# Products that nobody reads, in an attention + mixture-of-experts + MLP kernel: eight beside the first loads, four at the first unit's scores, and one at most transposings of the first batch

## The chip, the cores and the metric

The kernel runs on one core of one Trainium2 chip. The metric is the device time of one execution in microseconds (us); lower is better. PE is TensorE's matmul side (PEld its weight loads), DVE is VectorE, ACT is ScalarE, POOL is GpSimd, SP is SyncE, whose queue (SPq) issues the DMAs.

## What is computed

Three stages follow each other, all in f32 to the outside. Attention has 2 batches, 8 heads, 576 positions and 64 channels; it adds a local attention (a band of 3 positions to either side) and a coarse attention on means of 4 positions, repeated 4 times. Its output, as 1152 rows of 512, goes through 8 experts with balanced gates, and then through an MLP.

```python
def sm_attn(qq, kk, vv):
    s = scale * np.matmul(qq, kk.transpose(0, 1, 3, 2))
    s = s - np.max(s, axis=-1, keepdims=True)
    a = np.exp(s)
    a = a / (np.sum(a, axis=-1, keepdims=True) + 1e-09)
    return np.matmul(a, vv)
out_d = sm_attn(q_d, k_d, v_d)                  # q, k, v averaged over 4 positions
out_up = np.repeat(out_d, factor, axis=2)
scores = np.where(np.abs(pos[:, None] - pos[None, :]) < factor, scale * q @ k.T, -1e9)
...
attn_out = out_up + out_local
...
for e in range(E):                              # 8 experts, P: balanced gates
    h = np.maximum(x @ w1[e], 0.0)
    out += P[:, e:e + 1] * (h @ w2[e])
...
h = x @ w_in
g = np.maximum(h, 0.0) + np.log1p(np.exp(-np.abs(h)))
return g @ w_out
```

## The kernel before

**Units and blocks.** The attention runs over eight units, each of one batch and two heads: units 0 to 3 are batch 0, units 4 to 7 batch 1 (`units`, L660; the first argument of `Unit(n, b, u)` is the running number `n`). A unit has four blocks: "c", the coarse attention, and 0, 1 and 2, each with three tiles of 64 positions of the local one.

**The steps of a unit.** `load` (L492) has SP issue the DMAs of q and k into one tile `qk` (one buffer, L494, so that the next unit's q and k can come only once this unit's have been transposed), of v into `vw` and `vd`. `setup(g)` (L514, g = 0, 1, 2) transposes three tiles of `qk` on PE (`tb`, L523) and has DVE and ACT copy and reduce them into `qkd`, `kT`, `fine` and, at g = 2, `flat`. `scores(blk)` (L551) takes a PSUM bank `sc` and computes the scores: for "c" from `flat` and `qkd` (L557), otherwise first the mask by one bf16 product of the identity `identb` with 216 columns (L564) and then three tiles (L570). DVE takes the maximum (L577), ACT the exponentials (L582), DVE normalises into `ex` (L583 to L585). `turn(blk)` (L588) takes a bank `tp`, transposes `ex` on PE (L596 for "c", which has two halves c and a bank for each; L605 for the others) and ACT copies it out. `values(blk)` (L609) multiplies with v into a bank `pv` (L616, L627); DVE adds the coarse part (L642).

**PSUM.** `bank` (L489, L66) gives out eight banks. In batch 0 scores take m0, m1 and m2 in turn, `tb` and `tp` share four banks with the tag "at", and `pv` has the one bank "y". In batch 1 all the attention's banks are the four "at" banks, and the others serve the experts' products.

**Order.** The loop at L1028 writes the blocks of all units as one stream: at step n it writes the scores of block n, in the last two blocks of a unit the next unit's setup and then its successor's load, then the turn of block n-2 and the values of block n-3 (`LAG` is 2). From half of the stream on it puts the experts' first products (L831, L919) between, and operands and weights are made ready on DVE, ACT and POOL. Up to here the order on each engine is made by the program's scheduler from this order and from its own estimate of what is ready; it is fixed when the program is built, and each engine runs its queue in that order. From L1097 on the experts and the MLP follow in an order written out by hand.

`ident` (f32, L95) and `identb` (bf16, L458) are identity matrices; DVE writes `identb` near the start.

The lines of the main loop before the stream starts, and those that place a block:

```python
    blocks = ["c", 0, 1, 2]
    stream = [(x, blk) for x in units for blk in blocks]
    for g in range(NB):
        units[0].setup(g)
    units[1].load()
    ...
            x.scores(blk)
            ...
        for lag, what in ((LAG, "turn"), (LAG + 1, "values")):
            if 0 <= n - lag < len(stream):
                x, blk = stream[n - lag]
                getattr(x, what)(blk)
```

Of the kernel before, what the change touches and what calls it, by code (L numbers as in the profile page):

```python
# [20 lines left out]
def attention_moe_mlp(ctx: ExitStack, tc: tile.TileContext, q, k, v, w_gate, w1, w2, w_in, w_out, out):  # L21
    nc = tc.nc
    B, H, S, D = q.shape
    NT, DM = out.shape
    E, _, FF = w1.shape
    F2 = w_out.shape[0]
    P = 128
# [92 lines left out]
    class Job:  # L120

        def __init__(self, steps, rank, pace=None):
            self.begun, self.pace = order_.now, pace
            self.steps, self.rank, self.want, self.active, self.taken, self.done = steps, rank, None, False, {}, set()
            self.last = 0.0
            self.go(None)
# [331 lines left out]
    identb = ap.tile([P, P], BF16, bufs=1, name="identb")  # L458
# [4 lines left out]
    for t0, t1, off in ((0, 1, 0), (1, NB + 1, R), (NB + 1, NB + 2, 2 * R)):  # L463

        for hh in range(2):
            part = mask[hh * QT : (hh + 1) * QT, t0:t1, :]
            for sign in (1, -1):
                nc.gpsimd.affine_select(
                    out=part, in_=part, compare_op=ALU.is_gt, fill=NEG,
# [6 lines left out]
    for x in fine + flat:  # L476
        nc.gpsimd.memset(x, 0.0)

    class Unit:


        pairs = {}

        def __init__(self, n, b, u):
            self.b, self.u = b, u
            self.flat = flat[n % 2]
            self.state = {}

# [62 lines left out]
        def scores(self, blk):  # L551

            sc = self.bank("sc", 0)
            if blk == "c":
                rows, w = 2 * CT, SD
                for i in range(NB):
                    nc.tensor.matmul(  # L557
                        sc[:rows, i * w : (i + 1) * w], self.flat[:, i].rearrange("x h q -> x (h q)"),
                        self.qkd[:, :, 1], start=True, stop=True,
                    )  # L560
            else:
                rows, w = P, KW
                tiles = range(NB * blk, NB * blk + NB)
                nc.tensor.matmul(  # L564
                    sc[:, : NB * w], identb, mask[:, blk : blk + NB].rearrange("p t w -> p (t w)"),
                    start=True, stop=False,
                )
                for i, t in enumerate(tiles):
                    w0 = min(max(t * QT - R, 0), S - KW)
                    nc.tensor.matmul(  # L570
                        sc[:, i * w : (i + 1) * w], fine[blk][:, i].rearrange("x h q -> x (h q)"),
                        self.kT.rearrange("x t q -> x (t q)")[:, w0 : w0 + KW], start=False, stop=(i == NB - 1),
                    )
            scv = sc[:rows, : NB * w].rearrange("p (i s) -> p i s", i=NB)
            small = ap.tile([P, 2, NB, 1], F32, tag="small", bufs=4, name="small")
            off, rs = [small[:rows, i] for i in range(2)]
            nc.vector.tensor_reduce(off, scv, axis=AX.X, op=ALU.max, negate=True)  # L577
            ex = ap.tile([P, NB * SD], F32, tag="ex", bufs=3, name="ex")[:rows, : NB * w]
            ex = ex.rearrange("p (i s) -> p i s", i=NB)
            total = sc[:rows, NB * SD : NB * SD + NB].rearrange("p (i s) -> p i s", s=1)  # L580
            for i in range(NB):
                nc.scalar.activation(scv[:, i], scv[:, i], AF.Exp, bias=off[:, i], accum_out=total[:, i])  # L582
            nc.vector.tensor_scalar(rs, total, EPS, None, op0=ALU.add)  # L583
            nc.vector.reciprocal(rs, rs)
            nc.vector.tensor_tensor(ex, scv, rs.to_broadcast([rows, NB, w]), op=ALU.mult)  # L585
            self.state[blk] = ex

        def turn(self, blk):  # L588

            ex = self.state[blk]  # L590
            if blk == "c":
                et = ap.tile([HC, 2, NB * 2 * CT], F32, tag="etc", bufs=1, name="etc")
                for c in range(2):
                    tp = self.bank("tp", 1)
                    for i in range(NB):
                        nc.tensor.transpose(  # L596
                            tp[:HC, i * 2 * CT : (i + 1) * 2 * CT], ex[:, i, c * HC : (c + 1) * HC],
                            ident[: 2 * CT, : 2 * CT],
                        )
                    nc.scalar.copy(et[:, c], tp[:HC, : NB * 2 * CT])  # L600
            else:
                et = ap.tile([KW, NB * P], F32, tag="et", name="et")
                tp = self.bank("tp", 1)
                for i in range(NB):
                    nc.tensor.transpose(tp[:KW, i * P : (i + 1) * P], ex[:, i, :], ident)  # L605
                nc.scalar.copy(et, tp[:KW, : NB * P])
            self.state[blk] = et
# [52 lines left out]
    units = [Unit(4 * b + i, b, u) for b in range(B) for i, u in enumerate((0, 2, 1, 3))]  # L660
# [353 lines left out]

    blocks = ["c", 0, 1, 2]
    stream = [(x, blk) for x in units for blk in blocks]
    for g in range(NB):
        units[0].setup(g)
    units[1].load()
# [77 lines left out]
    with tc.manual_schedule(engines=engines):  # L1097
# [3 lines left out]
        for n in range(BESIDE, len(steps)):  # L1101
            if n == CV:
                converting.append(order_.add(conversions(), 2))
            e, g, s, p = steps[n]
# [67 lines left out]
```

## Time and profile before

| | |
|---|---|
| time, median of 3 runs | 1078.72 us (1078.42 to 1078.95) |
| the profiled execution's own time | 1076.35 us |
| its span, first to last instruction | 1074.3 us |
| mean granted clock of TensorE over the span | 0.992 |
| busy: PE, PEld, DVE, ACT, POOL | 1047.9, 932.8, 698.1, 568.5, 556.9 us |
| instructions | 17657 |

The profile describes one execution. Busy times are sums over the whole span, so they mix the attention, which takes the first part of it, with the experts and the MLP, which take the rest. The chain of waits is the work that ended last, followed back from the last instruction; 82% of it is PE. The timeline lists instructions in order of time, runs of the same kind merged into one row with a count; the duration there is from the start of the first to the modelled end of the last, so neighbouring PE rows overlap a little. [...]

### The profile page before, as it was taken

What the parts mean: (1) busy time and instruction counts of PE and PEld (TensorE: products, weight loads), DVE (VectorE), ACT (ScalarE), POOL (GpSimd) and SP (SyncE); (2) the same over time, 40 slices, a digit from 0 to 9 for tenths busy, and PEclk for the clock granted to TensorE, in tenths of its full rate; (3) what the DMA queues carried; (4) which work ended last, traced back from release to release, by engine and by line L of the source; (5) the groups of instructions that cost most, each with busy time, mean ns of one, the idle gap of its engine ahead of it and who ended that gap; (6) DMA issues with size and microseconds to landing.
All of it is one profiled execution on the core that took longest, in us unless ns stands there. A gap on an engine that the chain in (4) does not pass through costs nothing.

```text
span 1074.3 us, 17657 instructions
## 1 busy us (share of the span) xinstructions
PE 1047.9 (98%) x6385; PEld 932.8 (87%) x6385; DVE 698.1 (65%) x1430; ACT 568.5 (53%) x1475; POOL 556.9 (52%) x575
## 2 busy tenths in 40 slices
PE   6989999999999999999999999999999999999998
PEld 5768888888989999898999989898988999789987
DVE  4797655776566566665656566565664778776765
ACT  4788634444444444454444444444454667676663
POOL 4567514477575565555556566664575412232221
PEclk9899989999999999999999999999999999999999
DMA  7553301122433334333333333343334473253112
GB/s 169 115 141 86 92 1 40 60 87 86 145 97 94 113 93 133 98 118 118 114 117 93 94 102 105 105 117 118 118 98 138 145 294 140 108 228 136 69 40 89
DMA packets 133495, 119.69 MB, mean 111 GB/s; under 512 B 35744, under 2 KB 111776, under 8 KB 133408
## 3 DMA queue, kind: packets, MB, share of 16 engines
q1 hardware_dynamic: 133408, 118.56, 35.6%
q8 instruction: 50, 0.82, 0.3%
q14 instruction: 37, 0.30, 0.1%
HBM read 93.11 MB, written 25.43 MB: 110 GB/s over the span
## 4 chain that ended last, share of the span: by engine, by line
PE 82%; DVE 9%; ACT 4%; POOL 1%; issue 1%; SPq 1%; DMA 1%; ACTq 0%
PE yps L919 40%; PE m L831 36%; DVE ab L798 1%; POOL ab L795 1%; DVE ab L791 1%; ACT one L793 1%; PE sc L570 1%; DVE xl L441 1%; DVE one L789 1%; PE tb L523 1%; PE tp L605 1%; DMA qk<-in_k 1%; PE pv L627 1%; SPq L499 1%; DVE c L850 1%
## 5 line engine op out<-in xcount | busy, mean ns | idle before, releaser
L831 PE MATMUL m<-xh,w1h 128*128 128x320 f32 (+1 forms) x1120 | 334.2, 299 | 3.6 <-DVE hl L770 1.6
L831 PE MATMUL m<-xh,w1l 128*128 128x320 f32 (+1 forms) x1120 | 332.8, 297 | 0.0
L831 PE MATMUL m<-xl,w1h 128*128 128x320 f32 (+1 forms) x1120 | 332.6, 297 | 0.0
L831 PEld LDWEIGHTS m<-xh,w1h 128*128 128x128 f32 x1120 | 212.6, 190 | 21.1 <-ACT t L843 3.5
L831 PEld LDWEIGHTS m<-xl,w1h 128*128 128x128 f32 x1120 | 212.7, 190 | 13.0 <-DVE xl L441 0.2
L831 PEld LDWEIGHTS m<-xh,w1l 128*128 128x128 f32 x1120 | 212.5, 190 | 0.3 <-issue 0.2
L919 PE MATMUL yps<-w2h,hh 128*128 128x512 f32 x502 | 198.9, 396 | 2.2 <-ACT hh L800 2.2
L919 PE MATMUL yps<-w2l,hh 128*128 128x512 f32 x502 | 198.2, 395 | 0.0
L919 PE MATMUL yps<-w2h,hl 128*128 128x512 f32 x502 | 196.0, 390 | 0.0
L919 PE MATMUL yps<-w2h,h 128*128 128x512 f32 x436 | 153.0, 392 | 0.1
L850 DVE TENSOR_TENSOR c<-m,t 128x256 f32<-128x256 f32 (+1 forms) x160 | 72.8, 455 | 113.8 <-PE m L831 67.5
L295 POOL TENSOR_TENSOR w1l<-sums,w1h 128x512 fp32r<-128x512 f32 x72 | 99.6, 1395 | 86.9 <-ACT w1h L293 75.3
L316 POOL TENSOR_TENSOR w2l<-raw,w2h 128x512 fp32r<-128x512 f32 x72 | 98.7, 1390 | 59.6 <-ACT w2h L314 56.1
L795 POOL TENSOR_TENSOR ab<-one,ab 128x320 f32<-128x320 f32 (+1 forms) x64 | 54.6, 855 | 143.6 <-ACT one L793 143.6
L768 ACT ACTIVATE hh<-c 128x256 fp32r<-128x256 f32 (+1 forms) x138 | 60.7, 445 | 128.5 <-DVE c L850 128.5
L949 DVE SCALAR_TENSOR_TENSOR acc<-yps,pr,acc 128x512 f32<-128x512 f32 x117 | 87.3, 746 | 55.2 <-PE yps L919 54.5
L770 DVE SCALAR_TENSOR_TENSOR hl<-c,hh 128x256 fp32r<-128x256 f32 (+1 forms) x138 | 94.7, 690 | 32.1 <-ACT hh L768 30.4
L919 PEld LDWEIGHTS yps<-w2h,hl 128*128 128x128 f32 x502 | 94.4, 188 | 21.7 <-DVE hl L802 0.2
L919 PEld LDWEIGHTS yps<-w2h,hh 128*128 128x128 f32 x502 | 94.7, 189 | 15.2 <-ACT hh L800 2.6
L843 ACT COPY t<-m 128x256 f32<-128x256 f32 (+1 forms) x160 | 63.4, 398 | 79.6 <-PE m L831 79.3
L919 PEld LDWEIGHTS yps<-w2l,hh 128*128 128x128 f32 x502 | 94.7, 189 | 10.9
L919 PEld LDWEIGHTS yps<-w2h,h 128*128 128x128 f32 x436 | 82.0, 188 | 15.2 <-ACT h L800 0.3
(136 smaller groups left out, 1653.6 us busy)
## 6 DMA issues: line engine op xcount, KB each, us to landing
raw<-in_moe_w SPq DMA_DIRECT2D x72, 256.0 KB
raw<-in_moe_w SPq DMA_DIRECT2D x36, 512.0 KB
w1h<-s_in SPq DMA_DIRECT2D x10, 896.0 KB
w1l<-s_in SPq DMA_DIRECT2D x10, 896.0 KB
raw<-in_moe_w_in SPq DMA_DIRECT2D x32, 256.0 KB
raw<-in_moe_w_out SPq DMA_DIRECT2D x16, 512.0 KB
w2l<-s_out SPq DMA_DIRECT2D x10, 512.0 KB
w2h<-s_out SPq DMA_DIRECT2D x10, 512.0 KB
```

Source lines behind the costliest of these rows:

```text
L295: behind(chain, nc.gpsimd.tensor_tensor(lo[:, part], sums, hi[:, part].bitcast(F32), op=ALU.subtract))
L316: behind(chain, nc.gpsimd.tensor_tensor(lo[:, i], raw[:, i], hi[:, i].bitcast(F32), op=ALU.subtract))
L441: nc.vector.tensor_tensor(xl[s][:, i, kk], src, xh[s][:, i, kk].bitcast(F32), op=ALU.subtract)
L499: nc.sync.dma_start(qk[w * QT : (w + 1) * QT, cut, hh], src[b, h0 + hh].rearrange("(t p) d -> p t d", p=QT)[:, cut],)
L768: nc.scalar.activation(hh, c, AF.Relu)
L770: nc.vector.scalar_tensor_tensor(out=hl, in0=c, scalar=0.0, in1=hh.bitcast(F32), op0=ALU.max, op1=ALU.subtract)
L795: nc.gpsimd.tensor_tensor(ab, one, ab, op=ALU.subtract)
L831: nc.tensor.matmul(b[:, :h], x[:, i, kk, :], y[s][:, i, kk, :], start=(not more and n == 0), stop=(n == 5), skip_group_check=more,)
L843: nc.scalar.copy(t, b[:, :h])
L850: nc.vector.tensor_tensor(c, b[:, :h], t, op=ALU.add)
L919: nc.tensor.matmul(y, a[:, f, tok], b[:, f, :], start=(start and m == 0), stop=(stop and m == 5))
L949: nc.vector.scalar_tensor_tensor(out=acc[t], in0=y, scalar=pr[:, t, e : e + 1], in1=acc[t], op0=ALU.mult, op1=ALU.add,)
```

## The change

A function `stir(out, times)` issues products on PE: `identb` as weights against `identb` repeated four times, bf16, 128 x 128 against 128 x 512 columns, each written with start and stop into a whole PSUM bank. Nothing reads what they write; the bank's real products, which come later, start anew. `Unit` now keeps its number `n`. There are 29 such products:

- 8 into a `pv` bank of unit 0, written ahead of unit 0's setup;
- 4 in unit 0's `scores`, one at the head of each block, into that block's `sc` bank;
- in `turn`, ahead of a block's transposes and into its `tp` bank: 5 in unit 0 (2 for "c", one for each of the others) and 4 in each of units 1 to 3 (one at the first half of "c", one for each of the others), 17 in all.

Units 4 to 7, the experts and the MLP get none.

```diff
+    def stir(out, times):
+        for _ in range(times):
+            nc.tensor.matmul(
+                out.rearrange("p (a c) -> p a c", c=P), identb, identb.unsqueeze(1).to_broadcast([P, 4, P]),
+                start=True, stop=True,
+            )
+
     class Unit:
...
         def __init__(self, n, b, u):
-            self.b, self.u = b, u
+            self.n, self.b, self.u = n, b, u
...
             sc = self.bank("sc", 0)
+            stir(sc, 1 if self.n == 0 else 0)
             if blk == "c":
...
                 for c in range(2):
                     tp = self.bank("tp", 1)
+                    stir(tp, 1 if self.n == 0 or self.n < 4 and c == 0 else 0)
                     for i in range(NB):
...
                 tp = self.bank("tp", 1)
+                stir(tp, 1 if self.n < 4 else 0)
                 for i in range(NB):
...
     stream = [(x, blk) for x in units for blk in blocks]
+    stir(units[0].bank("pv", 2), 8)
     for g in range(NB):
         units[0].setup(g)
```

## Rows read from the trace of the kernel before

**Rows 1.** The page: busy time by engine; TensorE's granted clock in 40 slices.

```profile
PE 1047.9 (98%) x6385; PEld 932.8 (87%) x6385; DVE 698.1 (65%) x1430; ACT 568.5 (53%) x1475; POOL 556.9 (52%) x575
...
PEclk9899989999999999999999999999999999999999
```

**Rows 2.** Stretches, cut where a unit's "c" transposes begin; columns as headed.

```profile
core 0: us, PE busy (x) PEld busy (x) DVE busy (x) ACT busy (x) POOL busy (x), PEclk, DMA share, GB/s
6.72:18.00 11.28, 8.37 (x36) 7.12 (x36) 7.42 (x20) 5.52 (x27) 3.17 (x7) 1.00 0.93 192
18.00:32.64 14.64, 13.75 (x95) 11.12 (x95) 7.32 (x28) 7.81 (x37) 5.32 (x10) 1.00 0.45 119
32.64:42.99 10.35, 8.78 (x95) 7.23 (x96) 8.16 (x30) 8.46 (x37) 2.63 (x5) 1.00 0.56 118
42.99:55.16 12.17, 12.17 (x71) 10.18 (x72) 8.91 (x27) 9.69 (x37) 11.35 (x13) 0.58 0.71 153
55.16:78.00 22.84, 17.91 (x178) 14.29 (x177) 21.66 (x66) 19.17 (x77) 15.41 (x18) 1.00 0.52 140
78.00:140.00 62.00, 61.99 (x538) 53.41 (x539) 41.30 (x119) 41.38 (x152) 35.19 (x38) 1.00 0.33 84
```

**Rows 3.** Stretches of one microsecond, same columns, where the granted clock changes.

```profile
42.00:43.00 1.00, 0.58 (x13) 0.47 (x13) 0.96 (x6) 0.59 (x4) 1.00 (x2) 1.00 0.03 8
43.00:44.00 1.00, 1.00 (x7) 0.99 (x8) 1.00 (x3) 0.19 (x1) 0.92 (x2) 0.51 0.21 47
...
53.00:54.00 1.00, 1.00 (x10) 0.93 (x8) 0.93 (x4) 0.93 (x5) 1.00 (x2) 0.87 0.78 217
...
152.00:153.00 1.00, 1.00 (x5) 1.00 (x6) 0.06 (x1) 0.17 (x1) 0.00 (x0) 0.63 0.08 16
```

**Rows 4.** The chain of waits in order of time: start, us, engine, tile, line, count.

```profile
24.59 0.18 PE sc L564
24.77 1.22 PE sc L570 x6
...
29.28 0.76 PE sc L570 x6
...
33.33 0.09 PE sc L564
33.43 0.64 PE sc L570 x6
...
34.43 0.60 SPq L499
...
36.44 3.61 DMA qk<-in_k
...
154.85 3.51 PE m L831 x12
...
162.75 2.92 PE m L831 x18
```

**Rows 5.** Timeline of PE: start, us, line, out<-in, shape, count, [idle before <-releaser].

```profile
6.72 2.15 PE L523 MATMUL tb<-ident,qk 128*128 128x128 f32 x9 [6.72 <-DMA vd<-in_v]
12.21 1.69 PE L557 MATMUL sc<-qkd,flat 128*96 128x144 f32 x6
18.00 1.15 PE L596 MATMUL tp<-ident,ex 96*72 96x96 f32 x6 [1.91 <-DVE ex L585]
36.90 0.92 PE L557 MATMUL sc<-qkd,flat 128*96 128x144 f32 x6
40.18 0.85 PE L523 MATMUL tb<-ident,qk 128*128 128x128 f32 x6 [0.68 <-DMA qk<-in_k]
```

**Rows 6.** Timeline of DVE, same columns, in the first 14 us.

```profile
1.74 0.21 DVE L459 CAST identb<-ident 128x128 bf16<-128x128 f32 x1
10.82 0.60 DVE L534 TENSOR_SCALAR flat<-qkd 64x144 f32<-64x144 f32 x2
13.93 1.18 DVE L577 TENSOR_REDUCE small<-sc 96x3 f32<-96x432 f32 x3 [1.90 <-PE sc L557]
```

## The prediction

> **What bounds the kernel now.** I read the page first: PE is busy 98% of the span, and its clock is granted in full except in two or three of forty slices [rows 1]. That leaves next to nothing to win in the experts and the MLP, and the change puts nothing there. So I cut the first 140 us into stretches [rows 2], each beginning where a unit's "c" block is transposed. From 78 to 140 us PE is busy 61.99 of 62.00: there it is the bound. From 55.16 to 78 DVE is busy 21.66 of 22.84: there DVE is. Before that no engine is full all the time, and the three unit-long stretches differ: 14.64, 10.35 and 12.17 us for nearly the same instructions (95, 95 and 71 products; some of the third stretch's stand later).
>
> The chain of waits says why [rows 4]. Six products of L570 take 1.22 us at 24.77 and 0.64 at 33.43; the mask's product 0.18 and 0.09. [...]
>
> In the stretch at full speed, 32.64 to 42.99, PE is busy only 8.78 of 10.35 [rows 2], and the chain runs through the one q/k buffer: transposes end, SP issues from 34.43, the last part takes 3.61 us from 36.44 to land [rows 4], and PE stands idle 0.68 until the next transposes at 40.18 [rows 5]. This 10.35 us is thus the floor that a full clock can give; more clock gives no more.
>
> **What the change removes, adds and moves.** It removes nothing. It adds 29 products, 512 bf16 columns each. No row shows this shape; the nearest is the mask's product, bf16 too, with 216 columns: 512/216 x 0.18 = 0.43 us at half speed, 512/216 x 0.09 = 0.21 at full [rows 4]. I take these as the price of one on PE's queue.
>
> (a) The eight in front. `identb` is there at 1.74 + 0.21 = 1.95 us [rows 6], and PE has nothing before the first transposes at 6.72, which wait for the load [rows 5]. 8 x 0.43 = 3.4 us end at 5.4. Three of the four at unit 0's scores find their banks free from the start (m0, m1, m2) and can follow: 1.3 more, to 6.7. The waiting for the first load hides all eleven. Should three slip behind the transposes, they cost at most 1.3.
>
> (b) The other 18: one at unit 0's last scores, 17 at the transposes. Unit 0's two at "c" fit into the 1.91 idle before 18.00 [rows 5]. Its other four stand in the stretch in which PE is busy 13.75 of 14.64 [rows 2]: on the path. Of unit 1's four, three (0.64) fit the 0.68 idle before 40.18; one is on the path. Unit 2's four stand where PE is busy 12.17 of 12.17: on the path. Unit 3's four lie beside the DVE-bound stretch: hidden. Nine on the path cost 9 x 0.21 = 1.9 us at full speed, and 8 x 0.43 + 0.2 = 3.6 if the clock stays as it was. All 18 on the path, which is the upper bound, would be 3.8 and 7.7.
>
> (c) What the clock gives, if full from the first transposes to 55. At the start, "c" scores begin at 12.21 and take 1.69, ending at 13.90; DVE waits for them 1.90 [rows 5, 6]. Their last input is there at 10.82 + 0.60 = 11.42, and at full speed they take 0.92 (the row at 36.90), so 12.34: 1.5 us. From 18.00, 14.64 becomes 10.35: 4.3. From 42.99, 12.17 becomes 10.35: 1.8. Together 7.6, less 1.9: 5.7 us. DVE (7.32 to 8.91) and ACT (7.81 to 9.69) fit under 10.35; POOL, with 11.35 of 12.17 in the third stretch [rows 2], does not, and if its weights came to be waited for, 1.0 of the 1.8 would be lost.
>
> (d) How much of that comes. Half a microsecond's product in about every third microsecond is little, and PE still waits from 13 to 18 for loads and for DVE. I expect the clock up early, lost for a while there or around 40, and regained sooner than the 11 and 10 us it takes now, since PE's queue holds more work in just these stretches. I put three quarters of the second and third term: 1.5 + 0.75 x 6.1 = 6.1; the nine products at full speed but for a quarter, 1.9 + 0.25 x 1.7 = 2.3. Net 3.8 us. The share is a judgement; its bounds are nothing and all.
>
> Whether the clock heeds the products in every run is the open point. The three times of the kernel before lie within 0.53 us of each other, so no scatter of its rise that matters shows. [...]
>
> (e) What lies behind. No line after unit 3 changes. The stretch from 55.16 is bound by DVE and the one from 78 by PE, both nearly without idle, so an earlier start carries through whole. A second fall of the clock, at 152 [rows 3], is on the path: twelve L831 products take 3.51 there, while eighteen take 2.92 shortly after [rows 4], so the twelve lose 1.56. It may move or vanish as everything shifts, and PE products beside it gain or lose as much again: plus or minus up to 2.5 us. Also, each engine's order is remade by the scheduler when instructions are added, which no row can price; I leave about 1 us to either side.
>
> The sum is made on the profiled execution: 1076.35 - 3.8 = 1072.5, with 2.05 around the span unchanged. The median lies 2.4 above that execution (1078.72), so I predict **1074.9**.
>
> **Rivals.**
> *All of it comes.* The clock stays full to 55: 5.7 us, 1073.0; with the fall at 152 gone as well, some 8, 1070.5. For: floors of DVE and ACT allow it. Against: the idle 1.91 at 18 and the idle before 43 [rows 3, 5], with only a product or two in each.
>
> *Little comes.* The clock rises early over unit 0's first scores and falls again in the waiting before 18, so that the first term (1.5) and a quarter of the others (1.5) meet some 3 us of added products; or the load of q/k and POOL take the place of PE as what is waited for. Net about 0: 1078.7. [...]
>
> *It is slower.* The added products sit on PE's path at half speed. This needs one thing: that the clock still rises only near 29 and still falls near 43. Then (b) stands alone: 3.6 us, 1082.3; it decides in favour of slower once less than about half of (c) comes. For: PE is the bound of both slow stretches, and in-order products in front of real ones delay them 0.43 each. Against: eight products in a row keep PE busy where it now does nothing, and ten busy microseconds were enough to raise the clock at 53 [rows 3].
>
> **How the numbers follow.** The forecast (2 to 5 us gained) has 0.45, all of it 0.17, little 0.25, slower 0.13. About 0.2%, or 2.2 us, is what a measurement of this kernel can tell from no change. Faster than 1076.6: nearly all of the first two, less the lower edge of the forecast, 0.59. Slower than 1080.9: 0.11. Same: 0.30. The range leaves out the last of the slower and of the full case: 1070.5 to 1080.2.
>
> **What would show it.** Right: eight products of some 0.43 between 2 and 5.4; the first transposes still near 6.7, but nine of them in about 1.1 instead of 2.15; "c" scores ending near 12.4; the stretch from the first to the second unit's "c" transposes near 11 to 12 instead of 14.64; six L570 products at 0.64 by 25. The first experts' products (L831) about 4 us earlier than 58. Wrong: L570 at 1.22 up to 29 (the clock did not heed the products); L523 waiting for a `tp` bank that an added product holds; SP's q/k issues no earlier than 21.2 and 34.4 although PE is faster; DVE with new idle between 55 and 78, which would mean that weights or loads, not DVE, are late next.

## The result, and the profile after

The change makes the kernel **slower**: 1082.4 us (median of 8 runs, 1079.88 to 1085.9) against 1078.47 of the kernel before (8 runs, the three known ones among them, 1075.66 to 1079.18), a ratio of 1.0054, interval 1.0036 to 1.0073. The ratio is not the quotient of these medians, which is 1.0036. Ratios go by fast runs alone: one execution of thin, 1096.68, and one of bef_as_front, 1100.13, lie more than 1.5% above the fastest of their kernel and stand in the medians only. I had predicted 1074.9, range 1070.5 to 1080.2: wrong sign, and outside the range. The profiled execution took 1084.53 us, with a span of 1082.4.

The page of after, busy time and clock in slices (compare [rows 1]):

```profile
PE 1055.3 (97%) x6414; PEld 935.2 (86%) x6414; DVE 702.8 (65%) x1430; ACT 566.8 (52%) x1475; POOL 555.9 (51%) x575
...
PEclk7979999999999999999999999999999999999999
```

PE has 29 instructions more, as written. The third slice has a lower clock than before's (7 against 9). The first can't be compared: in before the column gives 1.00 from 6.72 to 18 [rows 2], yet the nine first transposes take 2.15 us there [rows 5] and 1.17 in late_front below, so for before I go by the durations up to 29 us. The timeline of PE in after (columns as in [rows 5]) shows that the front does what I said it would:

```profile
2.00 3.59 PE L481 MATMUL pv<-identb 128*128 128x512 bf16 x8 [2.00 <-DVE identb L459]
5.38 1.49 PE L481 MATMUL sc<-identb 128*128 128x512 bf16 x3
6.66 1.62 PE L530 MATMUL tb<-ident,qk 128*128 128x128 f32 x9
...
11.83 2.84 PE L578 MATMUL sc<-kT,fine 128*128 128x72 f32 x12 [3.36 <-ACT fine L548]
14.46 1.69 PE L565 MATMUL sc<-qkd,flat 128*96 128x144 f32 x6
...
59.15 1.18 PE L605 MATMUL tp<-ident,ex 96*72 96x96 f32 x6 [2.79 <-DVE ex L593]
...
63.09 0.56 PE L841 MATMUL m<-xh,w1h 128*128 128x256 f32 x1
```

Eleven products lie beside the first load at 0.43 each, the first transposes still start at 6.66, and nine of them take 1.62 instead of 2.15: the clock has risen. Then PE stands idle 3.36 us, the twelve score products take 2.84 again, and the "c" scores end at 16.15, where before they end at 13.90 [rows 5]. The lead is lost within ten microseconds. The first of the experts' products stands at 63.09, where it stood at 58.23 in before and I had said some 4 us sooner. In three stretches up to 55 us the clock is at half (columns as in [rows 2]):

```profile
11.00:18.00 7.00, 6.17 (x26) 5.34 (x26) 3.40 (x12) 2.35 (x13) 1.72 (x4) 0.51 1.20 215
21.00:28.00 7.00, 7.00 (x36) 5.26 (x36) 2.86 (x9) 3.34 (x13) 2.27 (x4) 0.52 0.67 146
35.00:38.00 3.00, 3.00 (x17) 1.90 (x17) 2.34 (x8) 2.36 (x10) 0.00 (x0) 0.50 0.41 94
```

Together they are some 17 us, where before had some 33 (from its first transposes at 6.72 to 29.3 by the durations [rows 4, 5], and from 43.0 to 53 by the column [rows 3]). So the clock was up for longer, much as I had said; the time did not follow. The stretches from one unit's "c" transposes to the next (columns as in [rows 2]; the fifth row runs on to 84):

```profile
0.00:19.96 19.96, 12.87 (x49) 8.44 (x49) 7.27 (x24) 6.46 (x28) 10.46 (x32) 0.83 0.87 175
19.96:33.66 13.70, 12.44 (x101) 9.73 (x101) 8.03 (x30) 7.78 (x37) 3.68 (x6) 0.75 0.41 91
33.66:45.55 11.89, 10.57 (x100) 8.24 (x100) 8.70 (x30) 8.80 (x39) 3.76 (x6) 0.86 0.49 105
45.55:59.15 13.60, 9.79 (x99) 7.71 (x99) 11.99 (x35) 10.42 (x44) 11.16 (x13) 0.99 0.73 166
59.15:84.00 24.85, 21.01 (x139) 17.43 (x140) 20.65 (x52) 15.54 (x57) 14.47 (x14) 0.71 0.41 105
...
147.00:180.00 33.00, 30.84 (x202) 27.05 (x202) 22.13 (x39) 16.87 (x43) 13.76 (x13) 1.00 0.07 21
```

The fourth row is the one to stop at. The clock is full (0.99) and the stretch takes 13.60 us, where before took 12.17 at 0.58: PE is busy only 9.79, DVE 11.99 against 8.91 [rows 2], and PE waits 2.79 for DVE before 59.15. In the fifth, the clock is at 0.71 where before had 1.00. Unit 5's "c" transposes start at 98.04 against 88.83. The added products are not what fills either row: in the fourth PE has 3.81 us to spare, and in the fifth the last of them is issued at 69.41, and the clock is still at 0.59 and 0.50 in the two stretches of 5 us from 75 on.

What did change there is the **order**. The scheduler places each engine's instructions from its own estimate, and with 29 more on PE it came out differently everywhere: of PE's 877 older instructions up to L1097, 484 stand at another position than before; 194 of DVE's 323, 185 of ACT's 308, 24 of POOL's 118, 31 of SP's 414.

### The profile page after: what moved, and what is told of

The parts are those of the page before. It is cut to its first block, busy times and chain, and to the rows that moved or that the text cites. A ratio compares the mean times of both kernels' runs of the same rounds, so it can differ in the third digit from the quotient of the medians.

```text
span 1082.4 us, 17701 instructions
## 1 busy us (share of the span) xinstructions
PE 1055.3 (97%) x6414; PEld 935.2 (86%) x6414; DVE 702.8 (65%) x1430; ACT 566.8 (52%) x1475; POOL 555.9 (51%) x575
## 3 DMA queue, kind: packets, MB, share of 16 engines
HBM read 93.11 MB, written 25.43 MB: 110 GB/s over the span
## 4 chain that ended last, share of the span: by engine, by line
PE 81%; DVE 9%; ACT 5%; POOL 2%; DMA 1%; issue 1%; SPq 1%; ACTq 0%; DVEq 0%; POOLq 0%
PE yps L929 40%; PE m L841 35%; DVE xl L441 2%; DVE ab L808 2%; POOL ab L805 1%; PE sc L578 1%; DVE ab L801 1%; ACT one L803 1%; DVE one L799 1%; PE tp L615 1%; DMA raw<-in_moe_w 1%; PE pv L637 1%; PE pv L626 1%; POOL sums L244 1%; DVE hl L812 1%
```

## The experiments

All ratios are to the kernel before, run beside them, with 95% intervals; u3 and u5 are the starts of unit 3's and unit 5's "c" transposes in the one profiled execution of each.

| kernel | order of the queues | products | median us | ratio | u3 | u5 |
|---|---|---|---|---|---|---|
| before | its own | 0 | | 1 | 55.16 | 88.83 |
| after | its own | 29 | 1082.4 | 1.0054 (1.0036 to 1.0073) | 59.15 | 98.04 |
| after_pin | own, start mended | 29 | 1082.81 | 1.0066 (1.0046 to 1.0085) | 58.86 | 97.72 |
| front_only | its own | 8 | 1083.9 | 1.0072 (1.0045 to 1.0099) | 53.59 | 91.98 |
| turns_only | its own | 17 | 1081.42 | 1.0033 (1.0011 to 1.0055) | 58.99 | 95.63 |
| thin | as after | 29, one weight column | 1089.71 | 1.0100 (1.0064 to 1.0136) | 65.99 | 106.37 |
| bef_chained | before's | 0 | 1077.46 | 0.9993 (0.9976 to 1.0009) | 55.20 | 89.15 |
| front_ord | before's | 8 | 1077.46 | 0.9999 (0.9980 to 1.0017) | 52.79 | 88.66 |
| after_ord | before's | 29 | 1079.16 | 1.0016 (0.9991 to 1.0041) | 54.91 | 90.02 |
| bef_as_front | front_only's | 0 | 1082.94 | 1.0059 (1.0034 to 1.0084) | 54.67 | 93.11 |
| bef_as_after | after's | 0 | 1085.59 | 1.0075 (1.0048 to 1.0103) | 58.53 | 93.83 |
| late_ord | before's | 16, elsewhere | 1077.57 | 0.9995 (0.9979 to 1.0011) | 55.83 | 89.37 |
| late_front | before's | 24, elsewhere | 1078.11 | 1.0002 (0.9982 to 1.0022) | 52.32 | 88.71 |
| gates_ord | before's | 8, in the gates | 1076.25 | 0.9989 (0.9976 to 1.0003) | 57.85 | 96.05 |
| as_after_again | after's | 0 | 1083.86 | 1.0072 (1.0046 to 1.0097) | 60.50 | 95.80 |
| as_after_pool | after's, POOL before's | 0 | 1085.63 | 1.0087 (1.0056 to 1.0118) | 62.64 | 97.44 |
| bef_pool_aft | before's, POOL after's | 0 | 1084.57 | 1.0074 (1.0050 to 1.0099) | 55.26 | 96.89 |
| after_pool | after's, POOL before's | 29 | 1082.94 | 1.0057 (1.0036 to 1.0079) | 59.46 | 95.98 |

**Is it the start?** In after DVE sums the gate weights (`wg`) ahead of unit 0's third reduction and waits 1.41 us for their load; in before the sum stands behind it and waits 0.38. My first theory was that this one instruction lost the front's gain. The row of after:

```profile
9.98 0.63 DVE L677 TENSOR_TENSOR wg<-wg 128x16 f32<-128x16 f32 x1 [1.41 <-DMA wg<-in_moe_w_gate]
```

after_pin puts the gate weights' three operations behind unit 0's setup:

```diff
+    with pinned(("Activation", "DVE")):
+        nc.vector.tensor_tensor(wg[:, 0], wg[:, 1], wg[:, 2], op=ALU.add)
+        nc.scalar.copy(wgs[:, :, :, :E], wg)
...
```

> The changed kernel with one thing more: DVE's and ACT's three instructions on the gate weights (wg) are queued behind all of unit 0's setup; all 29 products stay. Order theory (the loss comes from the scheduler's new order: in the changed kernel DVE waits 1.41 us for wg's load ahead of unit 0's third reduction, PE idles 8.5 to 11.8 and the clock falls at 11.5): the first scores begin near 9 instead of 11.83, unit 0's c transposes near 17 instead of 19.96, and the time lies 2.5 to 4 us under the changed kernel's, ratio to the kernel before 1.000 to 1.003. Load theory (the added products cost their own time on PE's queue, the order is incidental): the early start is given back, ratio 1.0045 to 1.0055.

The timeline of PE in after_pin:

```profile
9.76 1.56 PE L578 MATMUL sc<-kT,fine 128*128 128x72 f32 x12 [1.44 <-ACT fine L548]
11.15 0.92 PE L565 MATMUL sc<-qkd,flat 128*96 128x144 f32 x6
16.90 1.51 PE L530 MATMUL tb<-ident,qk 128*128 128x128 f32 x6 [4.82 <-DMA qk<-in_k]
...
19.97 1.18 PE L605 MATMUL tp<-ident,ex 96*72 96x96 f32 x6 [0.71 <-DVE ex L593]
```

The "c" scores now end at 12.07, a little ahead of the 12.34 I had worked out. And it is worth nothing: PE then waits 4.82 us for the next unit's q and k, and the "c" transposes start at 19.97, as in after. 1.0066: this theory fell.

**Which part?** Eight products in front alone; the 17 at the transposings alone; all 29 with a single weight column, in exactly the order of after.

```diff
-            stir(sc, 1 if self.n == 0 else 0)
-                    stir(tp, 1 if self.n == 0 or self.n < 4 and c == 0 else 0)
-                stir(tp, 1 if self.n < 4 else 0)
```

> Only the eight products in front, none at scores or transposes. DVE's order of the gate weights is that of the kernel before. Order theory and load theory both: nothing on PE's path, and the early clock gives what it can: ratio 0.998 to 1.000, nine first transposes in 1.6 or less instead of 2.15. If the early rise itself is without value because the clock falls again in the wait before unit 0's c transposes: 1.000.

```diff
-            stir(sc, 1 if self.n == 0 else 0)
-    stir(units[0].bank("pv", 2), 8)
```

> Only the 17 products at the transposes, none in front and none at the scores; the gate weights keep their place of before. Load theory: 17 of the 18 products that can lie on PE's path are here, so most of the loss is: ratio 1.0035 to 1.005. Order theory: the start is that of the kernel before, and the ratio is 0.999 to 1.0015.

```diff
-                out.rearrange("p (a c) -> p a c", c=P), identb, identb.unsqueeze(1).to_broadcast([P, 4, P]),
+                out[:1].rearrange("p (a c) -> p a c", c=P), identb[:, :1], identb.unsqueeze(1).to_broadcast([P, 4, P]),
```

> All 29 products, with one column of the identity as weights instead of 128, so that each writes one partition; 512 columns move as before. Every engine's order is that of the changed kernel. If the rises and falls of the clock in the changed kernel depend on the products' full width, the clock here rises later (first transposes at 0.24 each, like the kernel before) and the time is 1 to 3 us above the changed kernel's, 1.0064 to 1.008. If the width does not matter, or the clock gives nothing, 1.0054 as the changed kernel.

Each part alone is slower, each in an order of its own, so these runs don't tell a part from its order. turns_only by itself, with 1.0033, lies nearest to what the load theory expected (1.0035), and its twelve executions range from 1073.7 to 1083.33. front_only is the telling one, where both theories had expected a small gain or none: eight products, all hidden beside the first load (the first transposes start at 6.68), and 0.72% lost. The early clock did not come in its profiled execution: the nine first transposes take 2.15 us, as in before. Its stretches of 5 us at 70:

```profile
70.00:75.00 5.00, 3.84 (x18) 3.48 (x19) 5.00 (x16) 3.86 (x11) 1.63 (x2) 0.50 0.61 195
75.00:80.00 5.00, 5.00 (x27) 4.18 (x26) 3.56 (x14) 2.26 (x11) 0.87 (x2) 0.50 0.42 90
```

The clock is at half there, some 60 us after the last added product; unit 3 had begun 1.6 us ahead of before. thin, at the same order as after, was slower still by its median, but the two intervals overlap: that full-width products help in this order is pointed to, not shown. The first sign of it, a later rise of the clock, did not come: thin's nine first transposes take 1.17 us.

**The order or the products?** A kernel's queues can be held in another's order: at the end of the attention's code every engine's instructions are tied, neighbour to neighbour, without a semaphore, so that the scheduler has no choice left. The added products stand ahead of the instruction that they were written ahead of (the first eleven of after_ord at the head of PE's queue).

```diff
+            for k in order:
+                queue += ahead[plain[k].name] + [plain[k]]
+            for a, b in zip(queue, queue[1:]):
+                tc.add_manual_dep(
+                    b, a.name, mybir.DependencyInfo(mybir.DependencyClass.NoSync, mybir.DependencyReason.DATA),
+                    reason="queue",
+                )
```

front_ord and after_ord have the products of front_only and of after in the order of before; bef_as_front and bef_as_after have no product, in the orders of front_only and of after. bef_chained is the control: the kernel before, tied in its own order.

> The eight products in front alone, and each engine's queue chained in the order that it has in the kernel before, so that no other instruction stands elsewhere than there. Order theory (the products by themselves cost little; the loss of front_only, 1.0072, comes from the order that the scheduler made anew, above all in the second batch, where the clock falls between 55 and 85 us): the loss vanishes, ratio 0.998 to 1.001, and the clock stays full from 55 to 85. If the products do harm by themselves: 1.005 to 1.007 as front_only.

> No added product at all; each engine's queue chained in the order that it has in front_only, whose eight products are left out. Order theory: the loss is here without a single product, ratio 1.005 to 1.008, with the clock at half in much of 55 to 85 us. If the products do the harm: 0.999 to 1.001.

> All 29 products, each engine's queue otherwise chained in the order of the kernel before: the eight and the first three of the scores at the head of PE's queue, the other 18 directly ahead of the next product of their block. Order theory: ratio 0.996 to 1.000, with the start and the first three units 3 to 5 us ahead of the kernel before, as predicted for the change. Load theory (the 18 cost their time on PE's path): 1.002 to 1.005.

> No added product; each engine's queue chained in the order that it has in the changed kernel. Order theory: slower than the changed kernel or equal, since the order is the same and the early clock is missing: ratio 1.0054 to 1.011. If the products do the harm: 0.999 to 1.002.

> The kernel before with each engine's queue chained in the very order that it has, nothing added: the control of the chained kernels, and a second profile of that order. All theories: ratio 0.999 to 1.001. If the clock's falls differ from execution to execution of one order (the kernel before has ranged from 1072 to 1082 us here), this profile shows them at other places than the first profile, which had one between 43.0 and 53.2 and none from there to 152.

The table answers it. **The order alone costs 0.59 and 0.75%**, without one product; a second run of bef_as_after, as_after_again, gave 0.72%. **The products in the old order cost or bring nothing** that can be measured: 0.9999 and 1.0016. For all 29 that leaves room for a cost of up to 0.4%, the end of after_ord's interval, and its lead at unit 3 is 0.25 us, not the 3 to 5 that I had expected. In the new order, too, the products are not told from their absence: 1.0054 with them and 1.0075 and 1.0072 without, and the intervals overlap. Tying by itself is free (0.9993). bef_as_front in stretches of 5 us, with no product anywhere:

```profile
65.00:70.00 5.00, 3.30 (x38) 2.40 (x38) 4.97 (x11) 3.99 (x19) 4.92 (x7) 1.00 0.22 50
70.00:75.00 5.00, 3.67 (x16) 3.01 (x17) 5.00 (x13) 3.10 (x11) 2.80 (x3) 0.50 0.76 227
75.00:80.00 5.00, 5.00 (x26) 4.18 (x25) 4.47 (x15) 2.59 (x10) 0.45 (x2) 0.50 0.14 31
```

DVE is busy throughout (4.97, 5.00), PE waits for it, the clock falls, and the experts' first products then run at half speed. It is front_only's picture.

Why the old order gains nothing either is seen in front_ord. First its start, in the timeline of PE, and below it that of late_front, a later kernel with the same eight at the head of the same queue:

```profile
6.61 2.15 PE L536 MATMUL tb<-ident,qk 128*128 128x128 f32 x9 [1.01 <-POOL mask L473]
...
28.12 0.80 PE L583 MATMUL sc<-kT,fine 128*128 128x72 f32 x6
```

```profile
6.62 1.17 PE L536 MATMUL tb<-ident,qk 128*128 128x128 f32 x9 [1.03 <-POOL mask L473]
...
18.57 1.43 PE L584 MATMUL sc<-kT,fine 128*128 128x72 f32 x6
...
27.73 0.80 PE L584 MATMUL sc<-kT,fine 128*128 128x72 f32 x6
```

**The same eight products raised the clock in one execution and not in the other.** In front_ord the transposes take 2.15, as in before, and the score products are at the shorter time only from 28.12. In late_front the clock is up for the transposes (1.17), but down again at 18.57 and up only at 27.73. So little is gained early: unit 1's "c" transposes start at 31.54 and 31.15, against 32.64. From there on, front_ord in stretches of 5 us and in its timeline of PE:

```profile
50.00:55.00 5.00, 2.46 (x25) 2.04 (x27) 3.29 (x8) 3.86 (x19) 5.00 (x6) 0.94 0.58 185
55.00:60.00 5.00, 4.41 (x36) 3.47 (x33) 4.87 (x20) 4.89 (x21) 1.63 (x3) 0.50 0.49 121
60.00:65.00 5.00, 5.00 (x28) 4.12 (x27) 4.97 (x9) 3.10 (x12) 5.00 (x6) 0.54 0.48 104
```

```profile
52.79 0.41 PE L609 MATMUL tp<-ident,ex 96*72 96x96 f32 x3 [2.02 <-ACT sc L595]
```

Here the clock does not fall at 43, as it does in before [rows 3], but is at 1.00 from 45 to 50: from unit 2's "c" transposes (42.07) to unit 3's it takes 10.72 us instead of 12.17, and unit 3 starts 2.4 us earlier, after a wait of 2.02 us for ACT. The clock falls about 54 and stays down for some ten microseconds. **The fall was moved, not removed**, and at unit 5 the lead is 0.2.

**Can products keep the clock where it falls?** Still in before's order: two each at unit 3's transposings and unit 4's scores (late_ord); the same with the eight in front (late_front); and none of these, but four ahead of each half's logits in the gates, where the clock of before falls at 152 [rows 3] (gates_ord).

```diff
+            stir(sc, 2 if self.n == 4 else 0)
...
+                    stir(tp, 2 if self.n == 3 and c == 0 else 0)
...
+                stir(tp, 2 if self.n == 3 else 0)
```

> Order of the kernel before, and 16 products where DVE and not PE is the bound (55 to 75 us): two ahead of each of unit 3's transposings and two ahead of each of unit 4's scores; none elsewhere. Clock theory (the scatter of the kernel before and most of what the early lead lost in front_ord come from the clock falling in this stretch, where PE waits): the clock stays full from 55 to 80, the ratio is 0.995 to 0.999 and the runs scatter less. If the products' time on PE counts more: 16 x 0.21 = 3.4 us at most, 1.001 to 1.003.

> The same 16 products and the eight in front, in the order of the kernel before. In front_ord unit 3's c transposes began 2.4 us earlier than in the kernel before, but then the clock fell at 54 and the lead was gone by 89. Clock theory: the lead is kept, ratio 0.993 to 0.998. If the lead is lost to waiting for loads and DVE whatever the clock does: as late_ord.

```diff
+            stir(lg[:, P : P + HALF[s]], xh[s][:, 1, 0, :], 4)
             for t in TILES[s]:
                 o = t * P - T0[s]
```

> None of the change's products. Eight unread products instead at another place: in the gates, ahead of each half's logits (L690, small products that wait for ACT's copy L687), four of xh against itself (f32r, 128 weight columns, 256 or 320 columns) into the unused columns of the logits' bank; every engine's queue chained in the order of before. At 150 to 154 us the trace of before has PE idle 0.47 and eighteen small logits products, and the clock falls at 152; the chained control without a product shows no fall there and is 3.7 us shorter than before's profiled execution. Each of the eight takes 0.12 to 0.15 us at full clock by the L831 products of the same width, 1.1 together, of which the 0.47 can hide. Theory A (the weak work at the logits is what lets the clock fall, in a part of the executions, and products there keep it): clock 1.00 from 150 to 165 in the profile, time about 2 us under that of before at the median, ratio 0.997 to 0.9985, and a narrower spread of its runs. Theory B (the clock at 152 falls or not whatever PE does there, or it falls for the idle stretches further back): ratio 1.000 to 1.002, the cost of the products and no more, with a spread as wide as that of before.

None can be told from before; late_front leads by 2.8 us at unit 3 and by 0.1 at unit 5. The products at the transposings did not keep the clock there: it is at 0.50 from 55 to 60 us and at 0.66 from 70 to 75. late_ord has it in full from 55 to 80, but so has before. gates_ord has the lowest ratio, 0.9989, its interval reaching 1.0003. What they taught is about the clock itself. bef_chained, the kernel before in its own order, in stretches of 2 us:

```profile
152.00:154.00 2.00, 2.00 (x15) 1.77 (x14) 0.39 (x1) 1.15 (x4) 0.00 (x0) 1.00 0.03 8
154.00:156.00 2.00, 2.00 (x14) 2.00 (x14) 0.77 (x3) 0.14 (x1) 0.00 (x0) 1.00 0.00 0
```

No fall at 152 in this execution, with no product added; it took 1072.64 us where the profiled execution of before took 1076.35. So the full clock around the logits in gates_ord's profile (1.00 from 150 to 175) proves nothing for its products. That execution of gates_ord was its slowest (1081.25), and its start, which is the start of before, shows a part of why; the timeline of PE, the mask's products left out:

```profile
40.45 1.43 PE L582 MATMUL sc<-kT,fine 128*128 128x72 f32 x6
...
44.38 0.80 PE L582 MATMUL sc<-kT,fine 128*128 128x72 f32 x6
```

Six score products still take 1.43 at 40.45 and 0.80 only at 44.38: the clock rose some 13 to 15 us later than in before (29.28, [rows 4]), with the same queues and the same work. Unit 3 starts 2.7 us behind before, and unit 5 then 7.2, after another fall (0.50 from 60 to 70 us).

**What in the order costs it?** The timeline of DVE in after has one suspicious row, the first of these; POOL and ACT, from their timelines, stand below it:

```profile
67.65 3.74 DVE L441 TENSOR_TENSOR xl<-xf,xh 128x256 fp32r<-128x256 f32 x1
77.97 0.41 DVE L441 TENSOR_TENSOR xl<-xf,xh 128x256 fp32r<-128x256 f32 x1
...
80.75 0.41 DVE L441 TENSOR_TENSOR xl<-xf,xh 128x256 fp32r<-128x256 f32 x1
```

```profile
67.24 0.73 POOL L244 TENSOR_TENSOR sums<-raw 128x256 f32<-128x256 f32 x1
67.93 1.27 POOL L316 TENSOR_TENSOR w2l<-raw,w2h 128x512 fp32r<-128x512 f32 x1
69.16 0.73 POOL L244 TENSOR_TENSOR sums<-raw 128x256 f32<-128x256 f32 x1
69.85 1.27 POOL L316 TENSOR_TENSOR w2l<-raw,w2h 128x512 fp32r<-128x512 f32 x1
...
79.18 3.26 POOL L295 TENSOR_TENSOR w1l<-sums,w1h 128x512 fp32r<-128x512 f32 x1 [2.68 <-ACT w1h L293]
```

```profile
71.95 0.35 ACT L590 ACTIVATE sc<-sc,small 96x144 f32<-96x144 f32 x1 [2.85 <-DVE small L585]
```

A subtraction of the same shape takes 0.41 at 77.97, where POOL stands idle (2.68 before 79.18), and 3.74 at 67.65: the long one lasts until POOL's four instructions in a row are done (to 71.39 and 71.12), and ACT idles 2.85 behind it. POOL's queue differs from before's in 24 places, 11 of them among the twelve below. Four kernels, without a product but for the last, cross POOL's order with that of all other engines. Of POOL's queue, places 54 to 65 by their lines in the kernel before, as after has them (-) and as before does (+):

```diff
-L549 L549 L244 L316 L244 L316 L548 L548 L244 L244 L295 L295
+L316 L244 L316 L549 L549 L244 L244 L244 L295 L548 L548 L295
```

> No product, every queue chained in the order of after: the same kernel as bef_as_after, as the control of this comparison. Expected 1.006 to 1.009 of before again, an xl subtraction (L446) of some 3.7 us at about 65 on DVE while POOL is busy without a break, and unit 4's c transposes at about 77.6.

> No product, every queue in the order of after except POOL's, which is chained in the order of before (24 of 118 places differ; two w2l subtractions L321 and a sum L249 come ahead of v's sums L554 of the next unit instead of behind them, so that POOL works from 62 on, where after's order has it wait 2.8 us for PE, and is not in one unbroken stretch at 67). Theory A (the collision of DVE's xl subtraction with POOL's unbroken work is a main cost of the new order): no DVE subtraction of 128x256 over 2 us, unit 4's c transposes 2 to 3 us earlier than in the control, ratio 1.004 to 1.0055 of before. Theory B (the loss is spread over PE's, DVE's and ACT's order and the clock; the collision is hidden or replaced): as the control, 1.006 to 1.009. A miss on the other side is possible: POOL's earlier work meets other DVE instructions.

> No product, every queue in the order of before except POOL's, which is in the order of after. Theory A: POOL's place alone makes DVE's subtractions collide, some of them over 1.5 us between 55 and 80, unit 4's c transposes 2 us or more behind 72.7 to 73.2, ratio 1.002 to 1.004. Theory B: DVE's order stands elsewhere against POOL's, nothing or under 0.1%: 0.999 to 1.001.

> The change as it is, all 29 products, every queue in the order of after except POOL's, in the order of before. Theory A: 2 to 3 us below the change's 1.0054, so 1.0025 to 1.004 of before, and no xl subtraction over 2 us. Theory B: 1.004 to 1.007, as the change.

This theory fell too, and usefully. as_after_pool has no such 3.74 any more, its longest subtraction is 2.17 at 81.09, and it is no faster (1.0087); after_pool stays where after is (1.0057), though it differs from after in one more thing: the first three products at the scores stand behind the first transposes (the first at 7.70) and not ahead of them. But bef_pool_aft, in which 24 places of POOL's queue are all that differs from before, loses 0.74%, more than either theory had allowed. Its timelines of PE, ACT and POOL:

```profile
77.00 0.90 PE L528 MATMUL tb<-ident,qk 128*128 128x128 f32 x3 [6.23 <-ACT et L611]
```

```profile
75.95 0.62 ACT L298 CAST w1h<-sums 128x512 fp32r<-128x512 f32 x1 [5.28 <-POOL sums L249]
```

```profile
73.03 1.40 POOL L553 TENSOR_TENSOR vd<-vd 72x256 f32<-72x256 f32 x2 [5.18 <-DMA vd<-in_v]
```

Read upwards: POOL's queue now has v's sums ahead of a weight's sum, and waits 5.18 us for v's load; ACT, whose queue has the weight's cast next, waits for that sum; PE waits 6.23 for the copy behind the cast; and the clock is at half when PE starts again (0.50 from 75 to 80). In these runs the queues fit each other as a set: POOL's alone, put into the wrong set, costs as much as the exchange of all five, and POOL's queue of before, put into after's set, mends nothing. Which of the moved instructions of after's order costs most is left open. DVE's, ACT's, PE's and SP's orders were not exchanged singly.

## Why the prediction was wrong

**(a) and (b), the prices: right.** 0.43 at half speed for the shape, worked out from the mask's product; measured 3.59 for eight, 1.49 for three. Hidden beside the first load, as said. What the products at the transposes cost was never seen singly, but after_ord bounds it: with all 29 in the old order, 1.0016, 1.7 us by its middle and 4.4 by the end of its interval.

**(c), the clock's gain: right in its first term in after_pin and in its third in front_ord, wrong as a sum.** I took 10.35 us as what each unit takes at full clock. In the old order that nearly held for the third term (10.72 in front_ord), but the second never came there: the clock rose only near 28, and from unit 0's to unit 1's "c" transposes it took 13.71. In after a unit at 0.99 took 13.60, since DVE was late; in after_pin the 1.5 us at the start ran into a wait for q and k; in front_ord PE waited 2.02 us for ACT ahead of unit 3, and the lead of 2.4 was gone by unit 5. My own rival "little comes" had this: the load, or another engine, takes PE's place. For the products alone it was the right case: 1078.7 there, 1077.5 and 1079.2 in the old order.

**(d), the share: failed for the time, and for the clock it is a matter of the execution.** In after the clock did about what I had said (some 17 us at half up to 55 instead of some 33), and unit 3 began 4.0 us later all the same. Three quarters of the gain were to come, 3.8 us net; front_ord and after_ord give -0.2 to +0.4% between the ends of their intervals, with middles at 0 and +1.7 us. I argued from three runs within 0.53 us that the rise doesn't scatter. Single executions of the kernel before, in all these comparisons, lie between 1071.87 and 1081.77, and in one order the clock rose near 29 (before) or near 43 (gates_ord), and fell at 152 (before) or didn't (bef_chained); the transposes behind the eight in front took 1.17 in late_front and 2.15 in front_ord. Three close times had told me nothing of where the clock rises.

**(e), what lies behind: the step that failed and decided the sign.** I wrote that the scheduler remakes each engine's order, that no row can price it, and then gave it 1 us to either side. It costs 6 to 8: 1.0059, 1.0075 and 1.0072 without a product. "An earlier start carries through whole" also failed. In the old order the leads at unit 3, 2.4 us in front_ord and 2.8 in late_front, are 0.2 and 0.1 at unit 5. In after, 4.0 of the 9.2 us by which unit 5 is late are lost ahead of unit 3's "c" transposes and 5.2 behind them, where the change adds only unit 3's four products. The stretches there show a busy DVE and a fallen clock; which of the two takes the lead away was not tested. The fall at 152 did vanish in after (clock 1.00 from 147 to 180), within the 2.5 I had set aside, and did not save it.

**The rival "slower"** gave 1082.3, nearly the measured 1082.4, by a mechanism that did not happen: it needed the clock to rise only near 29 and to fall near 43, with the products as the cost. In after the clock rose beside the first transposes and was full from 45.55 to 58, and the order without a product costs as much. That the number is right is luck.

## What to carry to other kernels

Where a scheduler orders the queues, compare the order before and after an insertion, on every engine, before anything else: the eight and the 29 unread products brought orders that cost 0.59 and 0.75% without them (bef_as_front, bef_as_after). To measure an edit by itself, tie all queues in the old order. And a faster start in a stretch with several nearly full engines is worth what the next engine's wait leaves of it (0.2 of 2.4 us at unit 5 in front_ord); follow it to the first stretch that one engine fills before counting it.

## What the runs showed of the hardware that I had not expected

With identical queues the clock's rise differed by some 13 to 15 us between two executions (before at 29.28, gates_ord between 40.45 and 44.38), the same eight products ahead of the first transposes raised it in one and not in another (1.17 us for nine in late_front, 2.15 in front_ord), and one fall, at 152, was there in one and not in the next: a trace of one execution shows one draw of it.

A DVE subtraction of 128x256 f32 took 0.41 us beside an idle POOL (after, 77.97), 3.74 beside four POOL instructions in a row (67.65), and 0.41 again at 80.75, where POOL's instruction is the long one: 3.26, where one of the same line and shape takes 1.43 at 75.07. What made either of them long, no run here shows.
